# A gated mix of linear attention and a ReLU layer: first x chunk and W1 by plain loads, x transposed on TensorE, and other PSUM banks for nd and finA

## The chip, the cores and the metric

The kernel runs on one core of a Trainium2 chip. A core has five instruction queues that run side by side: TensorE (PE) multiplies matrices, VectorE (DVE), ScalarE (ACT) and GpSimd (POOL) work elementwise, and SyncE (SP) here only issues DMA transfers. ACT and POOL issue some transfers too. A queue works in order: an instruction that waits for a semaphore holds up all that stand behind it. The metric is the device time of one execution in microseconds (us); the runs of a kernel are summed up by their median.

## The reference

For x of 2048 rows and 512 columns (bf16) the output is g * a + (1 - g) * b, row by row:

```python
g = _sigmoid((x * gate_w).sum(-1, keepdims=True))
# a: linear attention, 32 heads of width 16
q, k, v = heads(x @ wqkv)
pq, pk = q @ w_phi, k @ w_phi                       # per head
phi_q = concat(softmax(pq), softmax(-pq))           # 32 features per head
phi_k = concat(softmax(pk), softmax(-pk))
kv, z = phi_k^T @ v, sum_s(phi_k)                   # over all 2048 rows
a = ((phi_q @ kv) / (phi_q . z + 1e-6)) @ wo
# b: dense layer
b = relu(x @ w1) @ w2                               # inner width 1376
```

The sums kv and z go over all rows, so no output row of a can be made before the last row of x has been through the first half.

## The kernel before

The 2048 rows are 16 tiles of 128 (index m), or 4 chunks of 512 (index c). XT holds x transposed, in four slabs of 128 columns of x (index s or dt); HT holds relu(x @ w1) transposed, in 10 full slabs of 128 (index kt) and a remainder of 96.

The order of the work on every engine is written out by hand. A small planner (`_Plan`) appends instructions to one list per engine, each with the events that it waits for; nothing is reordered later. PSUM has 8 banks, and the dictionary `free` remembers for each bank which event frees it.

The head. SP issues four transposing loads of chunk 0 (L138, events x00 to x03), then two of the q and k columns of wqkv (L141, wqk0 and wqk1), a plain load of the v columns (L143, wv), and transposing loads of chunks 1 to 3 (L146). ACT issues W1 in five pieces (L151) and a sixth with the columns from 1024 on (L153, w1r). POOL makes small index tiles (L156 to L159), waits for x02 (L160), then fetches w_phi into WPS (L161) and gate_w (L163), and builds the block matrices Wbd from WPS (L166, L170). PE starts with 12 matmuls on constants (L191) and then makes eight units of chunk 0 at once, one per PSUM bank, slab by slab (L206, called from the end of the program). Each unit is a sum of four matmuls with 512 columns; ACT (L200) or DVE (L202) apply the relu. `pre` (L251) multiplies the q and k weights by Wbd, `rest` (L229) makes the 96 remaining columns and the gate, `vtile` (L314) a tile of v.

The middle. For each tile m, `atile` (L267) makes the logits of q and k, ACT exponentiates them (L278), DVE sums and inverts (L282 to L292), POOL normalises (L294 to L301), and a transposing DMA moves phi_q into PHQ. `kv` (L335) adds tile m - 3 to the sums in banks 6 and 7. The units of chunks 1 to 3 (L206) fill PE between them. Six units of chunk 3 are left for after the last attention tile, with the last three `kv` among and behind them; `gate` (L357 to L360) runs on DVE there.

The join and the tail. `kvfin` (L344, L348) moves the sums into KVNZ on DVE. `nd` (L367) multiplies a tile of PHQ by KVNZ into two banks from b0 on, DVE inverts (L373) and divides (L377), and a transposing DMA (L383) moves the tile into OT. `finB` (L392) makes b, 11 matmuls; `finA` (L401) makes a, 4 matmuls, which ACT scales by the gate (L406, into TFA); `comb` (L415) adds them on DVE and stores the tile (L420). The tail's loop at m issues nd(m + 2), finB(m + 1), finA(m), comb(m).

Of the kernel before, what the change touches and what calls it, by code (L numbers as in the profile page):

```python
# [5 lines left out]
ACT = mybir.ActivationFunctionType  # L6
# [51 lines left out]
def bass_gated_mix__linear_kernel_hedgehog__dense_activation_relu__prompt_kernel(  # L58
# [17 lines left out]
    P = 128  # L76
# [16 lines left out]
    with ExitStack() as es:  # L93
# [14 lines left out]
        KVNZ = E(nc.sbuf_tensor("KVNZ", [P, NG, 68], BF16))  # L108
        OT = E(nc.sbuf_tensor("OT", [P, NDT, S], BF16))
        HR = E(nc.sbuf_tensor("HR", [P, 2, 4, P], BF16))  # L110
        ROW8 = E(nc.sbuf_tensor("ROW8", [P, 8], I32))
        COL8 = E(nc.sbuf_tensor("COL8", [P, 8], I32))
        ROW64 = E(nc.sbuf_tensor("ROW64", [P, 64], I32))
# [9 lines left out]
        TFA = E(nc.sbuf_tensor("TFA", [P, 2, D], BF16))  # L123
        PS = E(nc.psum_tensor("PS", [P, 8, 512], FP32))

        WQKT = PHQ[:, :, S - 512:S]
        OTM = WQK[:, 0, 0:3 * D].rearrange("p (a b) -> p a b", a=3)
        OSB = WQK[:, 1, 0:3 * D].rearrange("p (a b) -> p a b", a=3)
# [5 lines left out]
        free = {b: [] for b in range(8)}  # L134


        for s in range(NDT):
            p.dma("sp", lambda e, s=s: e.dma_start_transpose(  # L138
                out=XT[:, s, 0:512], in_=x2[0:512, s * P:(s + 1) * P]), f"x0{s}", ev=f"x0{s}")
        for i in range(2):  # L140
            p.dma("sp", lambda e, i=i: e.dma_start_transpose(  # L141
                out=WQKT[:, 4 * i:4 * i + 4, :], in_=A_wqkv[:, i * D:(i + 1) * D]), f"wqk{i}", ev=f"wqk{i}")
# [6 lines left out]
        w1parts = [(0, 0, 512), (0, 512, 1024), (1, 0, 1024), (2, 0, 1024), (3, 0, 1024)]  # L149
        for i, (s, a, b) in enumerate(w1parts):  # L150
            p.dma("act", lambda e, s=s, a=a, b=b: e.dma_start(  # L151
                out=W1[:, s, a:b], in_=B_w1[s * P:(s + 1) * P, a:b]), f"w1{i}", ev=f"w1{i}")
        p.dma("act", lambda e: e.dma_start(  # L153
            out=W1[:, :, 1024:DFF], in_=B_w1[:, 1024:DFF].rearrange("(j p) n -> p j n", p=P)), "w1r", ev="w1r")
# [6 lines left out]
        p.dma("pool", lambda e: e.dma_start(  # L161
            out=WPS[:, :, :], in_=A_w_phi.rearrange("(g hl) r c -> (hl r) g c", g=NDT)), "wps", ev="wps")
        p.dma("pool", lambda e: e.dma_start(  # L163
# [5 lines left out]
        for gt in range(NDT):  # L169
# [3 lines left out]
                M8[:, :].unsqueeze(2).to_broadcast([P, 8, FE]), ALU.mult),  # L173
                after=["wd", "m8"], ev=f"wbd{gt}")

        p.op("dve", lambda e: e.tensor_single_scalar(ROW8[:, :], ROW8[:, :], 4, ALU.arith_shift_right),
             after=["iota"], ev="r8")
        p.op("dve", lambda e: e.tensor_single_scalar(ROW64[:, :], ROW64[:, :], 5, ALU.arith_shift_right), ev="r64")
        p.op("dve", lambda e: e.tensor_tensor(M8[:, :], ROW8[:, :], COL8[:, :], ALU.is_equal), after=["r8"], ev="m8")
        p.op("dve", lambda e: e.tensor_tensor(M32[:, :], ROW64[:, :], COL16[:, :], ALU.is_equal),  # L180
             after=["r64"], ev="m32")
        for b in range(NB):
            p.op("dve", lambda e, b=b: e.memset(
                EB[:, b, 0:3, :].rearrange("p a (g f) -> p (a g) f", f=DH)[:, :, FE:DH], 1.0), ev=f"cst{b}")
            p.op("dve", lambda e, b=b: e.memset(VS[:, b, :, 64:65], 1.0), ev=f"one{b}")
        for b in range(2):
            p.op("dve", lambda e, b=b: e.memset(HR[:, b, :, NR:P], 0.0), ev=f"hz{b}")


        for _ in range(12):  # L190
            p.op("pe", lambda e: e.matmul(PS[:, 7, :], ones[:, 0:P], ones, start=True, stop=True))  # L191

        def xready(c):
            return [f"x0{s}" for s in range(NDT)] if c == 0 else [f"x{c}"]

        def relu(c, kt, bank, eng):
            dst, src = HT[:, kt, c * 512:(c + 1) * 512], PS[:, bank, :]
# [7 lines left out]
        def hmm(c, kt, bank, s, after):  # L205
            p.op("pe", lambda e: e.matmul(  # L206
                PS[:, bank, :], W1[:, s, kt * P:(kt + 1) * P], XT[:, s, c * 512:(c + 1) * 512],
                start=(s == 0), stop=(s == NDT - 1)),
                after=after, ev=(f"h{c}_{kt}" if s == NDT - 1 else None))

        rot = [0]

        def nextbank():
            rot[0] += 1
            return 3 + (rot[0] - 1) % 3

        def hunit(c, kt, eng="act"):
            bank = nextbank()
            w = [f"w1{i}" for i in range(len(w1parts))] if kt < 8 else ["w1r"]
            for s in range(NDT):  # L220
                hmm(c, kt, bank, s, (xready(c) + w + free[bank]) if s == 0 else ())
            relu(c, kt, bank, eng)

        def rest(c):
            bank = nextbank()
            for i in range(4):
                for s in range(NDT):
                    t0 = c * 512 + i * P
                    p.op("pe", lambda e, i=i, s=s, t0=t0: e.matmul(  # L229
                        PS[:, bank, i * P:i * P + NR + 1], XT[:, s, t0:t0 + P], W1[:, s, KU * P:DFF + 1],  # L230
                        start=(i == 0 and s == 0), stop=(s == NDT - 1), skip_group_check=True),
                        after=(xready(c) + ["w1r", "gw"] + free[bank] if i == 0 and s == 0 else ()),
                        ev=(f"h{c}_r" if i == 3 and s == NDT - 1 else None))
            src = PS[:, bank, :].rearrange("p (i n) -> p i n", i=4)
            b = c % 2
            p.op("act", lambda e: e.activation(HR[:, b, :, 0:NR], src[:, :, 0:NR], ACT.Relu),
                 after=[f"h{c}_r"] + ([f"hr{c - 2}"] if c >= 2 else []), ev=f"rr{c}")
            p.op("act", lambda e: e.activation(
                EG[:, 4 * c:4 * c + 4].unsqueeze(2), src[:, :, NR:NR + 1], ACT.Exp, scale=-1.0), ev=f"eg{c}")
            free[bank] = [f"eg{c}"]  # L240
            p.dma("sp", lambda e: e.dma_start_transpose(
                out=HT[:, KU, c * 512:(c + 1) * 512].rearrange("p (i t) -> p i t", i=4),
                in_=HR[:, b, :, :].rearrange("p i n -> p (i n)")), f"hr{c}", after=[f"rr{c}", f"hz{b}"], ev=f"hr{c}")

# [116 lines left out]
                 after=["g"], ev="gt")  # L361

        def nd(m):
            b0 = 0 if m == 0 or m % 2 else 2
            after = [f"tq{m}", "kvz1"] + free[b0] + free[b0 + 1]
            for g in range(NG):
                p.op("pe", lambda e, g=g: e.matmul(  # L367
                    PS[:, b0 + g // 4, (g % 4) * GW:(g % 4) * GW + 68],
                    PHQ[:, g, m * P:(m + 1) * P], KVNZ[:, g, :], start=True, stop=True),
                    after=(after if g == 0 else ()), ev=(f"nd{m}" if g == NG - 1 else None))  # L370
            r = m % 2
            ob = m % 3
            p.op("dve", lambda e: e.reciprocal(  # L373
                RDEN[:, r, :].rearrange("p (g h) -> p g h", g=NG),
                bass.AP(tensor=PS, offset=b0 * 512 + 64, ap=[[EPS, P], [GW, NG], [1, HG]])),
                after=[f"nd{m}"], ev=f"rd{m}")
            p.op("dve", lambda e: e.tensor_tensor(  # L377
                OTM[:, ob, :].rearrange("p (g h d) -> p g h d", g=NG, h=HG),
                bass.AP(tensor=PS, offset=b0 * 512, ap=[[EPS, P], [GW, NG], [DH, HG], [1, DH]]),
                bass.AP(tensor=RDEN, offset=r * H, ap=[[2 * H, P], [HG, NG], [1, HG], [0, DH]]), ALU.mult),  # L380
                after=[f"rd{m}"] + ([f"to{m - 3}"] if m >= 3 else []), ev=f"om{m}")
# [29 lines left out]
        def comb(m, cs=slice(0, 512), tag="", eng="sp"):  # L411
            ob = m % 3
            bank = fbank[(m, tag)]
            n = cs.stop - cs.start
            p.op("dve", lambda e: e.scalar_tensor_tensor(  # L415
                out=OSB[:, ob, cs], in0=PS[:, bank, 0:n], scalar=OMG[:, m:m + 1],
                in1=TFA[:, m % 2, cs], op0=ALU.mult, op1=ALU.add),
                after=[f"fb{m}{tag}", f"ta{m}"] + ([f"out{m - 3}"] if m >= 3 else []), ev=f"cb{m}{tag}")
            free[bank] = [f"cb{m}{tag}"]
            p.dma(eng, lambda e: e.dma_start(out=o2[m * P:(m + 1) * P, cs], in_=OSB[:, ob, cs]),  # L420
                  f"out{ob}{tag}", after=[f"cb{m}{tag}"], ev=f"out{m}{tag}")
# [12 lines left out]
        rest(0)  # L434
        vtile(0, "dve")
        for i in range(4, 8):
            pre(i)
        vtile(1, "dve")
# [113 lines left out]
```

## Time and profile before

| | us |
|---|---|
| median of 4 runs | 157.27 |
| lowest to highest | 157.04 to 157.61 |
| the profiled execution | 157.04 |
| its span, first to last instruction | 155.1 |
| PE busy | 145.2 (94%) |
| DVE busy | 89.9 (58%) |
| ACT busy | 71.7 (46%) |
| POOL busy | 55.2 (36%) |

The profile shows one execution. Its table of slices cuts the span into 40 equal parts of 3.88 us; a digit is the busy share in tenths. The chain of work that ended last is followed back from the last instruction to what released it, step by step; a line of it gives the start in us, the duration in us, the engine, the tile and the line of the kernel. The timeline gives start, duration, engine, line, operation, output and input, and in brackets how long the engine had stood idle and for whom. Matmuls overlap: the mean duration of one (379 ns with 512 columns) is longer than the distance between two (0.215 us). PEld is the loading of a matmul's stationary operand, beside the matmuls. A row of a table by windows gives the stretch, its length, the busy time of PE, PEld, DVE, ACT and POOL with the number of instructions, the granted clock of PE, the busy share of the DMA engines, and GB/s.

When the transfers of the head were issued and had landed, in us:

| transfer | KB | issued | landed |
|---|---|---|---|
| x00, x01, x02, x03 (transposing) | 128 each | 0.7, 2.0, 3.3, 4.6 | 4.0, 8.1, 11.4, 11.6 |
| W1, five pieces | 128, 128, 256, 256, 256 | 0.8 to 2.7 | 2.9 to 9.2 |
| w1r | 352 | 3.4 | 11.1 |
| wqk0, wqk1 (transposing) | 512 each | 5.9, 11.2 | 13.9, 16.9 |
| WV | 512 | 13.7 | 18.3 |
| x1, x2, x3 (transposing) | 512 each | 14.4, 18.2, 20.3 | 20.5, 23.9, 25.5 |

### The profile page before, as it was taken

How to read it: one execution, taken by the hardware profiler on the slowest of the kernel's cores; microseconds unless marked ns; L12 is line 12 of the kernel's file. 1: busy time of each engine (PE TensorE's matmuls, PEld its weight loads, DVE VectorE, ACT ScalarE, POOL GpSimd, SP SyncE). 2: the span in 40 equal slices, each digit the busy share in tenths (PEclk: the TensorE clock that was granted, in tenths of full speed). 3: DMA queues.
4: the chain of work that ended last, by engine and by line, in shares of the span. 5: the costliest groups of instructions: out<-in, count | busy, mean ns of one | idle time of the engine just before them, and what ended most of it. 6: DMA issues, size and time to landing. Idle time of an engine off the chain costs nothing.

```text
span 155.1 us, 2475 instructions
## 1 busy us (share of the span) xinstructions
PE 145.2 (94%) x950; PEld 71.9 (46%) x967; DVE 89.9 (58%) x146; ACT 71.7 (46%) x111; POOL 55.2 (36%) x63
## 2 busy tenths in 40 slices
PE   7959699999999999999999999699999999999973
PEld 3323464444544544444554545344454444444432
DVE  2204370878886876868678893744444555554432
ACT  0304456777777777878777763011122211111150
POOL 1004400587866876878877881000000000000000
PEclk9999999999999999999999999999999999999999
DMA  5999996032449686423244432143233322333222
GB/s 132 208 215 222 263 178 135 0 68 68 39 100 277 165 216 86 68 68 70 68 72 101 98 71 68 34 87 86 72 68 88 81 68 68 72 80 90 68 68 68
DMA packets 46602, 16.09 MB, mean 104 GB/s; under 512 B 40976, under 2 KB 46208, under 8 KB 46592
## 3 DMA queue, kind: packets, MB, share of 16 engines
q1 hardware_dynamic: 45136, 14.49, 43.8%
q10 hardware_dynamic: 1392, 1.44, 4.5%
q8 instruction: 7, 0.11, 0.3%
q0 software_dynamic: 64, 0.02, 0.1%
q14 instruction: 3, 0.02, 0.1%
HBM read 3.88 MB, written 2.10 MB: 39 GB/s over the span
## 4 chain that ended last, share of the span: by engine, by line
PE 81%; DMA 5%; ACT 4%; issue 3%; POOL 2%; SPq 2%; DVE 1%; POOLq 0%
PE PS L392 24%; PE PS L267 17%; PE PS L206 15%; PE PS L401 9%; PE PS L314 7%; DMA XT<-in_A_x_dram 5%; ACT EB L278 4%; PE PS L367 3%; PE PS L335 2%; SPq L138 2%; PE PS L229 1%; PE PS L251 1%; POOL Wbd L170 1%; DVE WQK L415 1%; POOL WPS L161 1%
## 5 line engine op out<-in xcount | busy, mean ns | idle before, releaser
L392 PE MATMUL PS<-W,HT 128*128 128x512 bf16 (+4 forms) x181 | 39.8, 366 | 0.3
L206 PE MATMUL PS<-XT,W 128*128 128x512 bf16 x155 | 37.9, 380 | 2.1 <-DMA XT<-in_A_x_dram 1.6
L294 POOL TENSOR_TENSOR EB<-EB,SC 128x1024 bf16<-128x1024 bf16 x16 | 30.8, 1928 | 22.8 <-DVE SC L285 22.8
L278 ACT ACTIVATE EB<-PS 128x960 bf16<-128x960 f32 x32 | 29.4, 970 | 15.5 <-PE PS L267 15.5
L406 ACT ACTIVATE TFA<-PS,GT 128x512 bf16<-128x512 f32 x16 | 11.0, 687 | 45.4 <-PE PS L401 45.4
L267 PE MATMUL PS<-WQK,XT 128*128 128x480 bf16 x128 | 28.6, 367 | 0.5 <-ACT EB L278 0.4
L282 DVE TENSOR_REDUCE ZB<-EB 128x64 f32<-128x1024 bf16 x16 | 19.5, 1220 | 15.7 <-ACT EB L278 15.7
L415 DVE SCALAR_TENSOR_TENSOR WQK<-PS,OMG,TFA 128x512 bf16<-128x512 f32 (+2 forms) x17 | 12.2, 719 | 27.3 <-ACT TFA L406 26.2
L200 ACT ACTIVATE HT<-PS 128x512 bf16<-128x512 f32 x36 | 21.1, 607 | 12.4 <-PE PS L206 12.3
L206 PEld LDWEIGHTS PS<-XT,W 128*128 128x128 bf16 x160 | 15.2, 98 | 20.7 <-DMA XT<-in_A_x_dram 2.6
L392 PEld LDWEIGHTS PS<-W,HT 128*128 128x128 bf16 (+1 forms) x187 | 16.9, 97 | 16.9
L267 PEld LDWEIGHTS PS<-WQK,XT 128*128 128x128 bf16 x128 | 11.9, 98 | 15.4 <-ACT EB L278 3.4
L287 DVE TENSOR_REDUCE ZB<-EB 128x64 f32<-128x1024 bf16 x16 | 18.6, 1161 | 0.0
L301 POOL TENSOR_TENSOR EB<-EB,SC 128x512 bf16<-128x512 bf16 x16 | 16.9, 1055 | 1.3
L401 PE MATMUL PS<-WO,OT 128*128 128x512 bf16 x63 | 16.2, 378 | 0.9 <-ACT TFA L406 0.9
L314 PE MATMUL PS<-WV,XT 128*128 128x512 bf16 x59 | 15.3, 378 | 0.4 <-issue 0.2
L377 DVE TENSOR_TENSOR WQK<-PS,RDEN 128x512 bf16<-128x512 f32 x16 | 11.1, 692 | 0.5
L401 PEld LDWEIGHTS PS<-WO,OT 128*128 128x128 bf16 x64 | 6.2, 97 | 8.7 <-issue 1.3
L285 DVE RECIPROCAL SC<-ZB 128x64 f32<-128x64 f32 x16 | 8.8, 553 | 0.5
L324 ACT ACTIVATE VS<-PS 128x512 bf16<-128x512 f32 x14 | 8.5, 605 | 0.0
L367 PEld LDWEIGHTS PS<-KVNZ,PHQ 128*128 128x128 bf16 x128 | 6.0, 97 | 4.7 <-issue 1.4
L367 PE MATMUL PS<-KVNZ,PHQ 128*128 128x68 bf16 x128 | 6.5, 194 | 1.3 <-DVE WQK L377 1.3
(43 smaller groups left out, 73.0 us busy)
## 6 DMA issues: line engine op xcount, KB each, us to landing
out_dram<-WQK SPq DMA_DIRECT2D x15, 128.0 KB, 1.7
W<-in_B_w_dram ACTq DMA_DIRECT2D x3, 256.0 KB, 5.8
W<-in_B_w_dram SPq DMA_DIRECT2D x1, 768.0 KB, 4.9
WV<-in_A_wqkv_dram SPq DMA_DIRECT2D x1, 512.0 KB, 4.6
W<-in_B_w_dram SPq DMA_DIRECT2D x1, 512.0 KB, 5.9
WO<-in_A_wo_dram SPq DMA_DIRECT2D x1, 512.0 KB, 3.8
W<-in_B_w_dram ACTq DMA_DIRECT2D x1, 352.0 KB, 7.7
W<-in_B_w_dram ACTq DMA_DIRECT2D x2, 128.0 KB, 2.4
```

The lines of the kernel that those rows point to most:

```text
L200: p.op("act", lambda e: e.activation(dst, src, ACT.Relu), after=[f"h{c}_{kt}"], ev=ev)
L206: p.op("pe", lambda e: e.matmul(PS[:, bank, :], W1[:, s, kt * P:(kt + 1) * P], XT[:, s, c * 512:(c + 1) * 512], start=(s == 0), stop=(s == ...
L267: p.op("pe", lambda e, dt=dt, which=which: e.matmul(PS[:, which, 0:DE], XT[:, dt, m * P:(m + 1) * P], WQK[:, which, dt * DE:(dt + 1) * DE] ...
L278: p.op("act", lambda e, s=s, o=dsts[s]: e.activation(o, src, ACT.Exp, scale=(1.0 if s == 0 else -1.0)), after=[f"qk{m}"] + busy, ev=f"{nm} ...
L282: p.op("dve", lambda e: e.tensor_reduce(ZB[:, b, 64:128], EB[:, b, 2, :].rearrange("p (g f) -> p g f", f=DH), AX.X, ALU.add), after=[f"em{ ...
L287: p.op("dve", lambda e: e.tensor_reduce(ZB[:, b, 0:64].rearrange("p (h s) -> p h s", s=2), bass.AP(tensor=EB, offset=base, ap=[[EBS, P], [ ...
L294: p.op("pool", lambda e: e.tensor_tensor(EB[:, b, 3, :].rearrange("p (g f) -> p g f", f=DH), EB[:, b, 2, :].rearrange("p (g f) -> p g f", ...
L301: p.op("pool", lambda e: e.tensor_tensor(EB[:, b, 0, :].rearrange("p (h s f) -> p h s f", h=H, s=2)[:, :, 1, :], EB[:, b, 1, :].rearrange( ...
L314: p.op("pe", lambda e, dt=dt: e.matmul(PS[:, bank, :], XT[:, dt, m * P:(m + 1) * P], WV[:, dt, :], start=(dt == 0), stop=(dt == NDT - 1)), ...
L367: p.op("pe", lambda e, g=g: e.matmul(PS[:, b0 + g // 4, (g % 4) * GW:(g % 4) * GW + 68], PHQ[:, g, m * P:(m + 1) * P], KVNZ[:, g, :], star ...
L392: p.op("pe", lambda e, kt=kt, M=M: e.matmul(PS[:, bank, 0:n], HT[0:M, kt, m * P:(m + 1) * P], W2[0:M, kt, cs], start=(kt == 0), stop=(kt = ...
L401: p.op("pe", lambda e, t=t: e.matmul(PS[:, bank, :], OT[:, t, m * P:(m + 1) * P], WO[:, t, :], start=(t == 0), stop=(t == NDT - 1)), after ...
```

## The change

Chunk 0 of x is fetched by two plain loads on SP into the first columns of OT (under the name XS), which is not written otherwise until the tail. Each partition takes four neighbouring rows of x, so that tile m of the first four holds the rows 4p + m; the stores of these four tiles use the same order (`orow`). PE transposes the 16 blocks with an identity matrix, made by two iotas on POOL and a compare on DVE, into banks 0, 1, 2 and 7; DVE and ACT copy them to XT. W1 comes in four pieces by columns, w10, w11 and w13 on ACT and w12 on SP. SP, and POOL's fetch of WPS and gate_w, then wait for w12; all transposing loads stand behind that wait. PE runs 6 constant matmuls in place of 12.

The first four units of chunk 0 are made in two halves of 256 columns, the other six one after the other as whole units, their relus by ACT and DVE in turn. The tile v0 comes ahead of `rest`.

In the tail, kv of the last tile and `kvfin` come two units earlier, nd(0) comes ahead of finB(0) and nd(1) behind it, nd(2) behind finB(1); nd takes banks 0 and 1 for even tiles and 2 and 3 for odd ones; finA takes bank 6, but 2 and 0 for the last two tiles.

```diff
-        for s in range(NDT):
-            p.dma("sp", lambda e, s=s: e.dma_start_transpose(
-                out=XT[:, s, 0:512], in_=x2[0:512, s * P:(s + 1) * P]), f"x0{s}", ev=f"x0{s}")
+        xq = x2[0:512, :].rearrange("(p j) d -> p j d", j=4)
...
+        for i in range(2):
+            p.dma("sp", lambda e, i=i: e.dma_start(out=XS[:, 2 * i:2 * i + 2, :], in_=xq[:, 2 * i:2 * i + 2, :]),
+                  f"x0{i}", ev=f"x0{i}")
+        w1cuts = [0, 256, 512, 1024, DFF]
+
+        def load_w1(eng, i):
+            a, b = w1cuts[i], w1cuts[i + 1]
+            p.dma(eng, lambda e: e.dma_start(
+                out=W1[:, :, a:b], in_=B_w1[:, a:b].rearrange("(j p) n -> p j n", p=P)), f"w1{i}", ev=f"w1{i}")
+
+        load_w1("act", 0)
+        load_w1("act", 1)
+        load_w1("sp", 2)
+        load_w1("act", 3)
+        p.wait("sp", ["w12"])
...
-        p.wait("pool", ["x02"])
+        p.wait("pool", ["w12"])
...
+        for _ in range(6):
+            p.op("pe", lambda e: e.matmul(PS[:, 7, :], ones[:, 0:P], ones, start=True, stop=True))
...
+        for j in range(4):
+            bank = (0, 1, 2, 7)[j]
+            tp = PS[:, bank, :].bitcast(BF16)[:, 0:512]
+            for dt in range(NDT):
+                p.op("pe", lambda e, tp=tp, j=j, dt=dt: e.transpose(
+                    tp[:, dt * P:(dt + 1) * P], XS[:, j, dt * P:(dt + 1) * P], IDN[:, :]),
+                    after=["idn", f"x0{j // 2}"], ev=(f"xt{j}" if dt == NDT - 1 else None))
...
-        for _ in range(12):
-            p.op("pe", lambda e: e.matmul(PS[:, 7, :], ones[:, 0:P], ones, start=True, stop=True))
...
         def nd(m):
-            b0 = 0 if m == 0 or m % 2 else 2
+            b0 = 2 * (m % 2)
...
-        for s in range(NDT):
-            for u in range(8):
-                w = f"w1{s + 1}" if s else f"w1{u // 4}"
-                hmm(0, u, u, s, [f"x0{s}", w])
-                if s == NDT - 1:
-                    relu(0, u, u, ("act", "dve")[u % 2])
-        hunit(0, 8)
-        hunit(0, 9)
+        for hf in range(2):
+            for u in range(4):
+                hmm(0, u, 3 + u, slice(hf * 256, hf * 256 + 256), [f"xc{2 * hf}", f"xc{2 * hf + 1}"] + w1of(u),
+                    f"h0_{u}" if hf else None)
+        for u in range(4):
+            relu(0, u, 3 + u, ("act", "dve")[u % 2])
+        for u, bank in zip(range(4, KU), (7, 0, 1, 3, 4, 5)):
+            hunit(0, u, ("act", "dve")[u % 2], bank)
         for i in range(4):
             pre(i)
+        vtile(0, "dve")
         rest(0)
-        vtile(0, "dve")
...
+            if i == 4:
+                kv(NT - 1)
+                kvfin()
             unit(*u)
-        kv(NT - 1)
-        kvfin()
+        nd(0)
         finB(0, 4)
-        nd(0)
         nd(1)
...
-            if m + 2 < NT:
+            if 2 <= m + 1 < NT - 1:
                 nd(m + 2)
             if m + 1 < NT - 1:
                 finB(m + 1, FB[(m + 1) % 3])
-            finA(m, 6 if m < NT - 1 else 2)
+            if m == 0:
+                nd(2)
+            finA(m, (6, 2, 0)[max(m - NT + 3, 0)])
```

More of the change, by code (lines that the diff above doesn't have):

```diff
@@ L110, in bass_gated_mix__linear_kernel_hedgehog__dense_activation_relu__prompt_kernel @@
         HR = E(nc.sbuf_tensor("HR", [P, 2, 4, P], BF16))
+        ROWI = E(nc.sbuf_tensor("ROWI", [P, P], I32))
+        COLI = E(nc.sbuf_tensor("COLI", [P, P], I32))
+        IDN = E(nc.sbuf_tensor("IDN", [P, P], BF16))
         ROW8 = E(nc.sbuf_tensor("ROW8", [P, 8], I32))
@@ L124, in bass_gated_mix__linear_kernel_hedgehog__dense_activation_relu__prompt_kernel @@
         PS = E(nc.psum_tensor("PS", [P, 8, 512], FP32))
+        XS = OT[:, :, 0:512]
         WQKT = PHQ[:, :, S - 512:S]
@@ L134, in bass_gated_mix__linear_kernel_hedgehog__dense_activation_relu__prompt_kernel, with orow @@
         free = {b: [] for b in range(8)}
-        for s in range(NDT):
-            p.dma("sp", lambda e, s=s: e.dma_start_transpose(
-                out=XT[:, s, 0:512], in_=x2[0:512, s * P:(s + 1) * P]), f"x0{s}", ev=f"x0{s}")
+        xq = x2[0:512, :].rearrange("(p j) d -> p j d", j=4)
+        oq = o2[0:512, :].rearrange("(p j) d -> p j d", j=4)
+        def orow(m):
+            return oq[:, m, :] if m < 4 else o2[m * P:(m + 1) * P, :]
+        for i in range(2):
[11 more added lines that the diff above has]
+        p.wait("sp", ["w12"])
         for i in range(2):
@@ L147, in bass_gated_mix__linear_kernel_hedgehog__dense_activation_relu__prompt_kernel @@
                 out=XT[:, :, c * 512:(c + 1) * 512], in_=x2[c * 512:(c + 1) * 512, :]), f"x{c}", ev=f"x{c}")
[L149 to L154, printed above, removed]
+        p.op("pool", lambda e: e.iota(COLI[:, :], [[1, P]], channel_multiplier=0))
+        p.op("pool", lambda e: e.iota(ROWI[:, :], [[0, P]], channel_multiplier=1), ev="iota0")
         p.op("pool", lambda e: e.iota(ROW8[:, :], [[0, 8]], channel_multiplier=1))
@@ L174, in bass_gated_mix__linear_kernel_hedgehog__dense_activation_relu__prompt_kernel @@
                 after=["wd", "m8"], ev=f"wbd{gt}")
+        p.op("dve", lambda e: e.tensor_tensor(IDN[:, :], ROWI[:, :], COLI[:, :], ALU.is_equal),
+             after=["iota0"], ev="idn")
         p.op("dve", lambda e: e.tensor_single_scalar(ROW8[:, :], ROW8[:, :], 4, ALU.arith_shift_right),
@@ L181, in bass_gated_mix__linear_kernel_hedgehog__dense_activation_relu__prompt_kernel, with xready @@
              after=["r64"], ev="m32")
+        for _ in range(6):
+            p.op("pe", lambda e: e.matmul(PS[:, 7, :], ones[:, 0:P], ones, start=True, stop=True))
+        def xready(c):
+            return [f"xc{j}" for j in range(4)] if c == 0 else [f"x{c}"]
+        for j in range(4):
[5 more added lines that the diff above has]
+                    after=["idn", f"x0{j // 2}"], ev=(f"xt{j}" if dt == NDT - 1 else None))
+            src = tp.rearrange("p (a b) -> p a b", a=NDT)
+            dst = XT[:, :, j * P:(j + 1) * P]
+            if j % 2 == 0:
+                p.op("dve", lambda e, s=src, d=dst: e.tensor_copy(d, s), after=[f"xt{j}"], ev=f"xc{j}")
+            else:
+                p.op("act", lambda e, s=src, d=dst: e.activation(d, s, ACT.Copy), after=[f"xt{j}"], ev=f"xc{j}")
+            free[bank] = [f"xc{j}"]
         for b in range(NB):
@@ L187, in bass_gated_mix__linear_kernel_hedgehog__dense_activation_relu__prompt_kernel, with w1of @@
             p.op("dve", lambda e, b=b: e.memset(HR[:, b, :, NR:P], 0.0), ev=f"hz{b}")
-        for _ in range(12):
-            p.op("pe", lambda e: e.matmul(PS[:, 7, :], ones[:, 0:P], ones, start=True, stop=True))
-        def xready(c):
-            return [f"x0{s}" for s in range(NDT)] if c == 0 else [f"x{c}"]
+        def w1of(kt):
+            return [f"w1{i}" for i in range(4) if w1cuts[i] <= kt * P < w1cuts[i + 1]]
         def relu(c, kt, bank, eng):
@@ L203, in relu @@
             free[bank] = [ev]
[L205 to L209, printed above, removed]
         rot = [0]
@@ L215, in nextbank, with hmm, hunit @@
             return 3 + (rot[0] - 1) % 3
-        def hunit(c, kt, eng="act"):
-            bank = nextbank()
-            w = [f"w1{i}" for i in range(len(w1parts))] if kt < 8 else ["w1r"]
+        def hmm(c, kt, bank, cols, after, ev):
             for s in range(NDT):
-                hmm(c, kt, bank, s, (xready(c) + w + free[bank]) if s == 0 else ())
+                p.op("pe", lambda e, s=s: e.matmul(
+                    PS[:, bank, cols], W1[:, s, kt * P:(kt + 1) * P],
+                    XT[:, s, c * 512 + cols.start:c * 512 + cols.stop],
+                    start=(s == 0), stop=(s == NDT - 1)),
+                    after=(after if s == 0 else ()), ev=(ev if s == NDT - 1 else None))
+        def hunit(c, kt, eng="act", bank=None):
+            bank = nextbank() if bank is None else bank
+            hmm(c, kt, bank, slice(0, 512), xready(c) + w1of(kt) + free[bank], f"h{c}_{kt}")
             relu(c, kt, bank, eng)
@@ L231, in rest @@
                         start=(i == 0 and s == 0), stop=(s == NDT - 1), skip_group_check=True),
-                        after=(xready(c) + ["w1r", "gw"] + free[bank] if i == 0 and s == 0 else ()),
+                        after=(xready(c) + ["w13", "gw"] + free[bank] if i == 0 and s == 0 else ()),
                         ev=(f"h{c}_r" if i == 3 and s == NDT - 1 else None))
@@ L419, in comb @@
             free[bank] = [f"cb{m}{tag}"]
-            p.dma(eng, lambda e: e.dma_start(out=o2[m * P:(m + 1) * P, cs], in_=OSB[:, ob, cs]),
+            p.dma(eng, lambda e: e.dma_start(out=orow(m)[:, cs], in_=OSB[:, ob, cs]),
                   f"out{ob}{tag}", after=[f"cb{m}{tag}"], ev=f"out{m}{tag}")
-        for s in range(NDT):
-            for u in range(8):
-                w = f"w1{s + 1}" if s else f"w1{u // 4}"
-                hmm(0, u, u, s, [f"x0{s}", w])
-                if s == NDT - 1:
-                    relu(0, u, u, ("act", "dve")[u % 2])
-        hunit(0, 8)
-        hunit(0, 9)
+        for hf in range(2):
[6 more added lines that the diff above has]
+            hunit(0, u, ("act", "dve")[u % 2], bank)
         for i in range(4):
             pre(i)
+        vtile(0, "dve")
         rest(0)
-        vtile(0, "dve")
         for i in range(4, 8):
```

## The prediction

> **What bounds the kernel now.** I read the table of slices first, then the chain of work that ended last in order of time, then the timeline where the chain leaves TensorE (PE). From 24 to 94 us and from 98 to 147 us PE never stops, and nothing there is edited; so the time can only be won or lost in the three thin places.
>
> ```profile
> PE   7959699999999999999999999699999999999973
> DMA  5999996032449686423244432143233322333222
> ```
>
> The head is the first six slices of 3.88 us: PE is partly idle while the DMA row stands at 9. The chain says what it waits for:
>
> ```profile
> 3.32 8.10 DMA XT<-in_A_x_dram
> 11.43 0.30 issue
> 11.72 0.91 POOL WPS L161
> ...
> 16.82 1.45 POOL Wbd L170 x4
> 18.27 0.14 issue
> 18.40 1.00 PE PS L251 x16
> ...
> 23.64 1.64 PE PS L267 x8
> ```
>
> The third transposing load of chunk 0 lands at 11.42. GpSimd (POOL) waits for exactly that one (x02) before it fetches WPS, so Wbd is ready at 18.27 and PE starts `pre` at 18.40. From there PE runs with only 0.17 us idle: `pre` 0-3 1.00, `rest` 0.69, V tile 0.86, `pre` 4-7 0.84, gap 0.17, V tile 0.81, h unit 0.86, until the first attention tile at 23.64, which is 5.24 after `pre` began.
>
> The join of the two halves of the kernel, and the end:
>
> ```profile
> 96.95 0.37 DVE RDEN L373
> 97.32 0.02 issue
> 97.34 0.70 DVE WQK L377
> 98.04 0.14 issue
> 98.18 0.67 PE PS L367 x16
> ...
> 147.58 0.70 ACT TFA L406
> 148.28 0.14 issue
> ```
>
> nd(1) writes the banks of nd(0), so PE stands from 96.92 (0.27 of nd(0) from 96.66) to 98.18, 1.26 us, while VectorE (DVE) divides tile 0. Near the end finA(14) shares bank 6 with finA(13) and waits for its eviction: the wait list gives PE 0.87 us there.
>
> **The head, part by part.** *Loads.* The plain loads up to w12 and w13 are 256 KB x 4, 512 and 352 KB: 1.93 MB. The same bytes needed until 11.4 us before: the windows give 218 GB/s from 2.0 to 11.4. Plain weight loads in this trace move faster:
>
> ```profile
> 2.00:11.40 9.40, 7.86 (x26) 2.75 (x24) 1.39 (x12) 1.28 (x1) 0.00 (x0) 1.00 1.15 218
> 48.00:52.00 4.00, 3.94 (x39) 2.38 (x39) 3.48 (x5) 3.09 (x6) 2.73 (x4) 1.00 1.11 354
> ```
>
> (the last column is GB/s; the second window is W2, 1 KB rows, from one queue). The new w10 and w11 have 512-byte rows, which no row of the trace shows, so I bound the rate: 205 GB/s (these 1.93 MB took the 9.4 us before) to 354, and take 325, near the plain row because no load in flight then transposes. Call T the landing of w12: 2.0 (first bytes; 0.74 to 2.0 carried 33 KB) + 1.93/0.325 = 7.9, with its receipt 8.0 (bounds 7.6 and 11.6). The Trainium skill, "DMA: Bandwidth & Descriptors", section "Issuing engines are not separate DMA queues", speaks against a gain from the second queue: all queues share the same 16 DMA engines, and only issue time is saved. The trace agrees: 354 GB/s came from one queue, and the loads before were on two queues already at 218. A sum by "two queues, twice the rate" would put T at 6.5; I leave T at 8.0, on the plain rate alone.
>
> *PE transposes.* x00 shares the engines with w10: 0.52 MB at 292 GB/s, the rate of the window from 2 to 3, is 1.8, so x00 at 3.8 and x01 at about 5.4. The identity costs two 128x128 iotas on POOL and one compare on DVE. The nearest rows are the 128x64 iotas (0.18, 0.19) and the compare of 128x64 (0.23); up to double each, ready by 2.0, hidden behind the load. The warm-ups give PE's cold pace: 12 of 512 columns start from 0.78 to 5.43, 0.423 apart, against 0.215 later (L392: 11 in 2.38). Six end at 3.4. A transpose of 128 columns is then 0.107 cold, 8 are 0.86: j 2 and 3 run from 5.4 to 6.3, where the W1 units can begin. The copies of j 0 and 1 (nearest row: 0.69 on DVE and 0.60 on ACT for 128x512) fit between 4.7 and 5.4; those of j 2 and 3 lie beside the first-half matmuls. The DVE fills of EB and VS, now behind two copies, end near 11.5, before DVE's first relu is wanted.
>
> *W1 units.* 32 matmuls of 256 columns at 0.108 plus 24 of 512 at 0.215 are 8.6 at full pace, as much as the 40 before: 6.3 + 8.6 = 14.9. But PE is cold:
>
> ```profile
> L191 PE MATMUL PS<-const-bfloat16-1.0 x12: 583/631/631, 0.8 to 5.4; 128*128 128x512 bf16 x12
> ```
>
> and L206's first matmul in the same view is 591 ns against a median of 379. The twelve warm-ups were followed by full pace at about 6.3, 5.5 us after they began. The Trainium skill, "TensorE: Matmul & The Clock Gate", Part 1, says the clock doubles after one whole busy window of 3.4 us and that the window runs free of the kernel; Part 4 adds that transposes do not count as busy. Six warm-ups (2.6 us) can't fill a window, so by the rule the units start cold and turn warm between 9.7 and 13.1. The trace shows only the late turn, consistent with a window from 2.9 to 6.3. By the row alone (5.5 us from 0.78, whatever ran) there is no penalty and the units end at 14.9; by the rule they lose half of 3.4 to 6.8 us, ending at 16.6 to 18.3. I take 17.2, nearer the rule, because PE will have stood idle twice in the window.
>
> *What `pre` then needs.* SP holds its transposing loads until T. Held behind that wait are wqk0, wqk1, WV, x1 to x3 and later hr0; POOL's WPS, gw, WD and Wbd wait for T as well. From the rows of 512 KB loads before: issue about 2.5 (L141's unqueued one 2.52), landing 5.2 after issue at best (L146), and then a spacing of 13.9 (25.5 - 11.6) over six loads, about 2.3. So wqk0 lands at T + 5.3 = 13.3, wqk1 at T + 7.9 = 15.9, WV at T + 9.4 = 17.4, x1 at T + 11.5 = 19.5. Wbd: 18.27 was 6.85 after x02, so T + 6.85 = 14.9; gw, 5.2 after, comes at 13.2. PE arrives at `pre` at 17.2 and finds all of it; the V tile, moved ahead of `rest`, is reached at 18.2, 0.8 after WV; the h unit of chunk 1 at 21.6, 2 us after x1. The first attention tile moves from 23.64 to 17.2 + 5.24 = 22.4: **1.2 us saved**. The floor is WV: even a warm PE waits for it at 17.4, then 4.3 of work: 21.7, at most 1.9 saved.
>
> **The join: 1.1 saved.** kv(15) needs the last GpSimd product, ready at 92.10; moved two units (1.72) earlier PE reaches it at 92.30, a margin of 0.2. kvfin (0.93) then queues behind the gate arithmetic on DVE, free at 93.47:
>
> ```profile
> 90.17 1.93 POOL L294 TENSOR_TENSOR EB<-EB,SC 128x1024 bf16<-128x1024 bf16 x1 [0.45 <-DVE SC L285]
> ...
> 92.45 1.02 DVE L360 TENSOR_SCALAR OMG<-GT 128x16 f32<-128x16 f32 x1
> ```
>
> so nd(0) can start at about 94.45, where PE is ready at 94.28: a new stall of 0.2. finB(0) (2.38) covers tile 0's division (1.09), and nd(1) has other banks. Removed 1.26, added 0.2.
>
> **The end: 0.25 saved.** With banks 6, 2 and 0, finA(14) follows at once, saving 0.87. What is late next is the transposed tile 15: SP issues it at 146.57 and such a DMA takes 2.4 in all but its contended cases, so 148.97, while finA(15) would be ready at 148.42. A stall of 0.6 is given back. Strided rows of the first four output tiles stay 128 rows of 1 KB, off the path.
>
> **Sum.** 157.04 (span 155.1 and 1.94 around it) - 1.2 - 1.1 - 0.25 = 154.5. The median of the runs is 0.23 above the profiled execution, so **154.7**.
>
> **Rivals.** *A, as worked out:* 154.7, chance 0.50. *B, the head gains nothing:* PE turns warm at 13.1 or later and reaches `pre` at 18.4 again, or WV keeps the V tile waiting; only the tail is left, 157.27 - 1.35 = 155.9. For it speaks the rule on transposes; against it that PE is steadily busy from 6.3. Chance 0.25. *C, warm at once:* PE waits for WV, head 1.9 and to15 a little sooner: 153.8, chance 0.08. *D, the held loads come too late:* at 205 GB/s T is 11.6, WV lands at 21.0, and the first attention tile moves to 25.3, 1.7 later, against 1.35 of tail: 157.6. PE, standing from about 18 to 21, may fall back to the cold pace, up to 1.7 more (half of 3.4): 158.4 in the middle. It decides once T passes 11.3. For it: small rows, and a mean of 218 before 11.4; against it: the 354 of plain loads. Chance 0.17. *That the hold does nothing* is part of A: bytes, not order, set T.
>
> **How the numbers follow.** A measurement of this kernel tells changes from none at about 0.3% (0.5 us). A, B and C are faster: 0.83. D splits into 0.05 within and 0.12 slower. The range is 153.4 (C's gain, with the join a little better) to 157.0 (B with a late WV); what it leaves out is D and a remainder of C.
>
> **What would show it.** Right: w12 landing near 8; W1 units from about 6.3; W1 matmuls of 256 columns about 0.21 apart at first and 0.11 later; `pre` at 16.5 to 17.5 with no wait on Wbd; no DVE piece between the nd tiles near 95; finA(15) waiting for a DMA. Wrong: V tile or `pre` waiting for WV or wqk, w12 after 10, W1 units starting after 7, or kv(15) waiting for GpSimd.

## The result, and the profile after

The changed kernel takes 156.81 us (median of 34 runs) against 157.46 us for the kernel before (55 runs). The ratio is 0.9948, with a 95% interval of 0.9933 to 0.9963: 0.8 us faster, where 2.5 us and 154.7 had been forecast. The ratio is of the fast runs alone: seven runs of the changed kernel and four of the other, more than 1.5% above the fastest of their kernel, are left out of it, and so the medians of all runs lie only 0.65 us apart. That 156.81 lies within the forecast range of 153.4 to 157.0 is luck: the cause was none of the four cases.

The profile shown here is of an execution of 158.39 us, in which TensorE (PE) fell to half its pace at the very end; in most executions it doesn't, and a second profile of the same kernel, after_again, used below, has it at full pace to the end.

The table of slices of the kernel after (40 slices of 3.91 us; PEclk is the granted clock in tenths, 9 being 90% or more):

```profile
PE   6799899999999999999999999999999999999593
PEclk9999999999999999999999999999999999999968
DMA  3949997028249696131324434143332224222611
```

The head is better filled than before (its first six slices read 6, 7, 9, 9, 8, 9 where they had read 7, 9, 5, 9, 6, 9), but the DMA row has a hole in its third slice, and PE now has a 5 in the third slice from the end, with a low clock behind it. Neither had been forecast. The chain of work that ended last, its lines for the head, the join and the end:

```profile
1.76 7.35 DMA W<-in_B_w_dram
9.11 0.02 issue
9.13 2.23 SPq L163
11.36 0.05 issue
11.40 2.42 SPq L163
13.83 0.04 issue
13.87 4.63 DMA WV<-in_A_wqkv_dram
18.50 0.05 issue
18.55 1.04 PE PS L351 x4
...
22.99 1.63 PE PS L304 x8
...
93.79 0.41 PE PS L404 x8
94.20 2.38 PE PS L429 x11
96.58 0.26 PE PS L404 x8
...
144.82 3.95 DMA OT<-WQK
148.77 0.05 issue
148.82 1.04 PE PS L438 x4
149.85 4.10 PE PS L429 x22
```

*Head.* The chain no longer goes through Wbd but through w12 (landed at 9.11), the held transposing loads, and WV at 18.50; PE had finished `pre` 0-3 and stood 0.68 us for it. The first attention tile begins at 22.99 in the chain, 0.65 earlier than before (22.82 in the timeline, which counts from the first matmul's start). *Join.* nd(0) and finB(0) follow one another with no DVE piece between the nd tiles, as forecast. *End.* The transfer of tile 15 into OT, to15, takes 3.95 us from its issue where it took 2.4 before, and finA(15) starts at 148.82. The last 22 matmuls then take 4.25 us in place of 2.57. PE's timeline of the kernel before and of the kernel after:

```profile
150.14 2.57 PE L392 MATMUL PS<-W,HT 128*128 128x384 bf16 x22
```

```profile
149.69 4.25 PE L429 MATMUL PS<-W,HT 128*128 128x384 bf16 x22
```

Where the time went, from the timelines of all profiles (us; a tile whose first matmul is missing from the records is counted from where that matmul belongs, 0.22 earlier). The first column is one execution each and scatters, since it hangs on transfers; the ratios carry the verdicts.

| kernel | first attention tile | from there to finA(0) | from there to the end of PE | PE waits before finA(15) | ratio to before |
|---|---|---|---|---|---|
| before | 23.48 | 77.6 | 51.6 | 0 (finA(14): 0.87) | 1 |
| after | 22.82 | 76.5 | 54.6 | 2.17 | 0.9948 |
| after_again | 23.10 | 76.5 | 52.6 | 1.84 | 0.9974 |
| head_only | 22.65 | 77.6 | 51.6 | 0 (finA(14): 0.87) | 0.9952 |
| tail_only | 24.22 | 76.5 | 51.4 | 0.64 | 0.9904 |
| tail_late | 23.11 | 76.5 | 54.9 | 2.48 | 1.0035 |
| fetch_early | 24.11 | 76.5 | 51.5 | 0.69 | 0.9902 |
| fetch_still | 23.26 | 76.5 | 53.1 | 2.26 | 0.9996 |
| no_hold | 21.84 | 76.5 | 54.9 | 2.47 | 0.9901 |
| no_hold_early | 22.14 | 76.5 | 51.5 | 0.68 | 0.9802 |
| b_first | 21.48 | 76.5 | 50.9 | 0 | 0.9771 |
| best | 21.37 | 76.5 | 50.9 | 0 | 0.9758 |

What made to15 late stands in the view of the DMA queues, cut to the 4 us in which it was in flight (kernel after; a line per queue gives packets, MB, and the share of 16 engines; a line per transfer its count and the us from issue to landing):

```profile
q1 hardware_dynamic: 797, 0.36, 65.6%
q8 instruction: 1, 0.02, 1.9%
out_dram<-WQK SPq DMA_DIRECT2D x2, 128.0 KB, 1.7
OT<-WQK SPq DMA_TRANSPOSE x1, 4.0
```

A single packet of the queue of kind "instruction" runs beside it. Over the whole program this queue had 7 packets before and 8 after, 16 KB each (packets, MB and share of the two pages, before and after), and the eighth falls between 146.0 and 146.5:

```profile
q8 instruction: 7, 0.11, 0.3%
```

```profile
q8 instruction: 8, 0.13, 0.4%
```

So theory F: to15 is late because the code of PE is fetched beside it, and the fetch stands there because the head's edits make PE's program 26 matmuls longer (78 in place of 52). Rival R: the new tail itself makes its transfers collide.

### The profile page after: what moved, and what is told of

It is laid out like the page before. It is cut to its first block, busy times and chain, and to the rows that moved or that the text cites. A ratio compares the mean times of both kernels' runs of the same rounds, so it can differ in the third digit from the quotient of the medians.

```text
span 156.3 us, 2530 instructions
## 1 busy us (share of the span) xinstructions
PE 147.5 (94%) x976; PEld 75.5 (48%) x993; DVE 91.8 (59%) x150; ACT 72.5 (46%) x112; POOL 55.6 (36%) x65
## 4 chain that ended last, share of the span: by engine, by line
PE 73%; DMA 10%; ACT 5%; DVE 5%; SPq 4%; issue 1%
PE PS L429 24%; PE PS L304 17%; PE PS L250 11%; PE PS L438 8%; PE PS L351 7%; ACT EB L315 5%; DMA W<-in_B_w_dram 5%; SPq L163 3%; DMA WV<-in_A_wqkv_dram 3%; PE PS L404 3%; DMA OT<-WQK 3%; PE PS L372 2%; PE PS L266 1%; DVE ZB L319 1%; DVE ZB L324 1%
## 5 line engine op out<-in xcount | busy, mean ns | idle before, releaser
L429 PE MATMUL PS<-W,HT 128*128 128x512 bf16 (+4 forms) x183 | 41.8, 378 | 0.2
L250 PE MATMUL PS<-XT,W 128*128 128x512 bf16 (+1 forms) x170 | 39.0, 372 | 0.3
L429 PEld LDWEIGHTS PS<-W,HT 128*128 128x128 bf16 (+1 forms) x187 | 17.5, 101 | 18.0 <-issue 1.7
L250 PEld LDWEIGHTS PS<-XT,W 128*128 128x128 bf16 x176 | 17.6, 103 | 16.7 <-DMA XT<-in_A_x_dram 0.5
L351 PEld LDWEIGHTS PS<-WV,XT 128*128 128x128 bf16 x64 | 5.4, 97 | 5.3 <-DMA WV<-in_A_wqkv_dram 0.8
```

Of the source, the lines that this page charges most:

```text
L250: p.op("pe", lambda e, s=s: e.matmul(PS[:, bank, cols], W1[:, s, kt * P:(kt + 1) * P], XT[:, s, c * 512 + cols.start:c * 512 + cols.stop], ...
L351: p.op("pe", lambda e, dt=dt: e.matmul(PS[:, bank, :], XT[:, dt, m * P:(m + 1) * P], WV[:, dt, :], start=(dt == 0), stop=(dt == NDT - 1)), ...
L429: p.op("pe", lambda e, kt=kt, M=M: e.matmul(PS[:, bank, 0:n], HT[0:M, kt, m * P:(m + 1) * P], W2[0:M, kt, cs], start=(kt == 0), stop=(kt = ...
```

## The experiments

**The tail alone.** The kernel before, with the edits to kv, kvfin, nd and finA only, none to loads, transposes or units:

```diff
-            b0 = 0 if m == 0 or m % 2 else 2
+            b0 = 2 * (m % 2)
...
-            finA(m, 6 if m < NT - 1 else 2)
+            finA(m, (6, 2, 0)[max(m - NT + 3, 0)])
```

> The kernel before with the tail's edits alone (kv and kvfin two units earlier, the order and banks of nd, banks 6, 2, 0 of finA); TensorE's program has as many instructions as before. Theory F (in the changed kernel the transfer of tile 15 into OT, to15, is late because a 16 KB code fetch of TensorE runs at 146.0 to 147.3, beside it; the fetch stands there because the head's edits add 26 matmuls to TensorE's program): no fetch near to15, which lands 2.4 us after its issue; join 1.05 and end 0.25 saved, 1.3 us in all, ratio to before 0.992. Rival R (the tail's own new order makes to15 collide with the stores of tiles 12 and 13): to15 takes about 4 us here too, finA(15) waits about 2.2 us, and at most 0.4 us are saved, ratio 0.997 to 1.000.

Ratio 0.9904 (0.9878 to 0.9931). The DMA view of this kernel over the 4 us from the issue of to15 has no packet of the instruction queue, and to15 lands after 2.4:

```profile
q1 hardware_dynamic: 794, 0.35, 33.0%
out_dram<-WQK SPq DMA_DIRECT2D x2, 128.0 KB, 1.7
OT<-WQK SPq DMA_TRANSPOSE x1, 2.4
```

The timeline of PE gives the wait that is left, 0.64 (0.6 was forecast):

```profile
148.69 1.04 PE L401 MATMUL PS<-WO,OT 128*128 128x512 bf16 x4 [0.64 <-DMA OT<-WQK]
```

Rival R falls: the new tail alone is worth more (1.5 us) than the whole change (0.8).

**The tail, and a longer program.** The same with 28 matmuls on constants behind the 12 of the start, where PE then waits for x anyway:

```diff
+        for _ in range(28):
+            p.op("pe", lambda e: e.matmul(PS[:, 7, 0:64], ones[:, 0:P], ones[:, 0:64], start=True, stop=True))
```

> The kernel before with the tail's edits, as tail_only, and 28 constant matmuls of 64 columns behind its 12 of the start. They end about 1.5 us later, before the second and third slab of x have landed (8.1 and 11.4 us), so the head should not move; but TensorE's eighth code fetch now comes near to15. Theory F: to15 takes 3.6 to 4 us, finA(15) waits about 2.2 us in place of 0.64, 1.5 us more than tail_only, ratio to before 1.000 in place of 0.990. Rival: matmuls that hide behind a load cost nothing wherever they move the fetch, 0.990.

Ratio 1.0035 (1.0010 to 1.0060), 0.0131 or 2.1 us more than without them. The head didn't get longer (first tile at 23.11), but now an eighth fetch stands at 146.0 to 146.5, and the DMA view around to15 reads:

```profile
q1 hardware_dynamic: 796, 0.36, 64.0%
q8 instruction: 1, 0.02, 2.4%
out_dram<-WQK SPq DMA_DIRECT2D x2, 128.0 KB, 2.0
OT<-WQK SPq DMA_TRANSPOSE x1, 4.3
```

In PE's timeline the same four matmuls wait 2.48 in place of 0.64:

```profile
149.41 1.59 PE L403 MATMUL PS<-WO,OT 128*128 128x512 bf16 x4 [2.48 <-DMA OT<-WQK]
```

Matmuls that do nothing and lie beside a load cost as much as the new tail had won: theory F. Only PE's program was made longer here, and the fetch came; so the packets of this queue are PE's code. The excess over the 1.5 forecast is the clock: in this execution too the granted clock fell to 0.50 (from about 149.7 to 153.2 us), and the mean clock shows such a fall in 8 of the 22 runs; the 14 others have a median of 157.42, beside 157.43 for the kernel before, which is the 1.000 of the forecast.

**The changed kernel with the fetch moved.** 12 matmuls of 64 columns, and as a control 3, behind the 6 of the start:

```diff
         for _ in range(6):
             p.op("pe", lambda e: e.matmul(PS[:, 7, :], ones[:, 0:P], ones, start=True, stop=True))
+        for _ in range(12):
+            p.op("pe", lambda e: e.matmul(PS[:, 7, 0:64], ones[:, 0:P], ones[:, 0:64], start=True, stop=True))
```

> The changed kernel with 12 more constant matmuls of 64 columns behind the 6 of the start, in the time in which TensorE waits for the first half of x (3.5 to 4.3 us). They add 24 instructions, so each code fetch comes about 12 matmuls (some 2.6 us) earlier in the tail, at about 143.4 to 144.7, between the transfers of tiles 14 and 15. Theory F: to15 lands 2.4 us after its issue, finA(15) waits about 0.6 us in place of 2.2; 1.5 us less than the changed kernel, ratio to before about 0.985. Rival R: nothing of the tail changes, ratio 0.995 as for the changed kernel, or more where the added matmuls cost time.

> The same with 3 constant matmuls of 64 columns: the fetch moves by about 0.6 us only and still meets to15. Theory F: to15 takes 3.3 to 4 us, ratio to before 0.993 to 0.996, as the changed kernel. Rival R2 (added matmuls gain by warming TensorE in the head, wherever the fetch stands): part of the gain of the run with 12 shows here too.

With 12 the last fetch moved to 142.5, to15 landed after 2.5, and finA(15) waited 0.69: the mechanism as expected. The time, 0.9902 (0.9870 to 0.9935), was 0.8 us short of it. In the profiled execution, the slowest of the six (156.68; the median is 156.08), WV landed late (PE waited 1.1) and x1 at 23.2 (0.6), and the first tile began at 24.11: what was gained at the end was lost again in the head, where the first fetch now stood at 20.3 beside x1. That the other five lost less of the same kind is likely, but not shown. With 3 the fetch stayed (146.5 to 147.0, to15 issued at 145.25) and the wait was 2.26; the ratio, 0.9996 (0.9956 to 1.0036), is even above that of the changed kernel, with runs from 156.5 to 159.7: the clock fell in 6 of the 12, and the 6 others have a median of 156.89, 0.9945 of the kernel before. So added matmuls as such gain nothing. The first tile's scatter, 22.65 to 24.11 in the kernels with the hold, suggests that the head had a problem of its own.

**The head alone.** The changed kernel with the old tail:

> The changed kernel with the tail as before: the head's edits alone, 26 more matmuls in TensorE's program than before. In the old tail finA(14) waits 0.87 us for ACT, so finA(15) comes later and covers part of a late to15. Theory F + H: first attention tile 0 to 0.8 us earlier, by when WV and x1 land (18.5 to 19.2 and 21.9 to 23.2 in the three runs with the hold); the fetch comes at about the end of to15's transfer and costs 0 to 0.7; ratio 0.996 to 1.001. As forecast before (head 1.2 us): 0.992.

Ratio 0.9952 (0.9934 to 0.9970), 0.76 us: a little better than the 0.996 to 1.001 expected, at the upper end of theory H, and not the 1.2 us of the forecast. The first tile began at 22.65, with a wait of 0.7 for WV. The fetch came at 148.5, when to15 (issued at 145.74) had landed, and cost nothing. Together the two halves alone make 0.0048 + 0.0096 = 0.0144; both at once measured 0.0052. The missing 0.0092, 1.4 us, is the fetch that neither half has at that place, and the fall of the clock behind it: no run of head_only or tail_only shows one, of 28.

**The hold taken away.** The changed kernel without SP's wait; POOL still waits for w12:

```diff
         load_w1("act", 3)
-        p.wait("sp", ["w12"])
```

> The changed kernel without SP's wait for w12; POOL's wait for w12 stays. Theory H (the hold leaves the DMA engines empty for some 2 us, from 8.4 to 10.7 us in the profile, and so WV lands at 18.5 and x1 at 21.9, for which TensorE waits 0.7 and 0.5 us): w12 still lands near 9, wqk0, WV and x1 about 2 us earlier, both waits go, the first attention tile starts about 0.9 us earlier, ratio 0.995 - 0.006 = 0.989 to before. Rival B (the order of the transfers doesn't matter, or the transposing loads push W1 back): W1 lands 1 us or more later, TensorE waits for w12 or w13 among the W1 units, ratio 0.995 or more.

Ratio 0.9901 (0.9871 to 0.9931), with the late to15 still in it (a wait of 2.47). The table by windows of the kernel after and of this one, for the same 2.3 us (the last column is GB/s):

```profile
8.40:10.70 2.30, 2.30 (x16) 1.78 (x15) 0.64 (x6) 0.12 (x1) 1.29 (x2) 1.00 0.06 17
```

```profile
8.40:10.70 2.30, 2.30 (x21) 1.95 (x19) 0.76 (x6) 0.42 (x1) 0.93 (x2) 1.00 1.28 258
```

With the hold the DMA engines move 17 GB/s while SP waits for w12's receipt and then for its first transposing load to start; without it 258. w12 landed 0.36 us later (at 9.47), not the 1 us or more of rival B, and PE waits for no W1 piece among the units. WV was issued at 12.3 in place of 13.9, no wait of PE for WV or x1 is left, and the first tile begins at 21.84. Rival B falls.

**Both causes removed.** The 12 small matmuls and no hold:

> The changed kernel without SP's wait for w12 and with 12 constant matmuls of 64 columns in the gap at the start. If both causes stand and add up: head 1.6 us (first attention tile at 22.0 as in no_hold), join 1.05, end 0.25, 2.9 us in all, and finA(15) waits 0.65 us: ratio to before about 0.981. If the two runs before shared one cause, 0.990 as each of them.

Ratio 0.9802 (0.9775 to 0.9829), 3.1 us faster than before. Both marks are there, the first tile at 22.14 and a wait of 0.68 before finA(15), so these are two causes and not one. Against the changed kernel's 0.9948 this is 0.0146, more than the 0.0046 and 0.0047 that the two edits brought alone: the run with 12 matmuls had lost time in the head, and no_hold still had the late to15.

**The changed kernel again,** beside the last three on one chip:

> The changed kernel itself, beside the others on one chip: ratio 0.993 to 0.997; TensorE's eighth code fetch near 146, to15 landing 3.6 to 4 us after its issue, a wait of about 2.2 us before finA(15), WV landing at 18.5 to 19.2.

Ratio 0.9974 (0.9940 to 1.0008), within the interval's reach of the first. Its DMA view around to15, and PE's wait:

```profile
q8 instruction: 1, 0.02, 1.2%
out_dram<-WQK SPq DMA_DIRECT2D x2, 128.0 KB, 1.7
OT<-WQK SPq DMA_TRANSPOSE x1, 3.6
```

```profile
148.77 1.04 PE L438 MATMUL PS<-WO,OT 128*128 128x512 bf16 x4 [1.84 <-DMA OT<-WQK]
```

The clock stayed up here (0.999 over the span), so the late transfer is no product of the execution shown above; the fall of the clock is a second price on it. The mean clock of every run is on record: it is below 0.995 in 27 of the 89 runs of kernels whose to15 is late (after, after_again, tail_late, fetch_still, no_hold), and in 4 of 126 of the others, the kernel before among them.

**A better version.** First the small piece of finB(15) into the wait that is left; then, besides, 8 matmuls of 512 columns and 8 of 64 at the start, and 2 of 512 between the groups of transposes:

```diff
+            if m == NT - 1:
+                finB(m, 3, slice(384, 512), "b")
             finA(m, (6, 2, 0)[max(m - NT + 3, 0)])
...
-        for i, cs in enumerate(cuts):
-            finB(m, (4, 3)[i], cs, "ab"[i])
-        for i, cs in enumerate(cuts):
-            comb(m, cs, "ab"[i], ("sp", "act")[i])
+        finB(m, 4, cuts[0], "a")
+        comb(m, cuts[1], "b", "act")
+        comb(m, cuts[0], "a", "sp")
```

> no_hold_early with the small last piece of finB(15) (128 columns, 11 matmuls, about 0.6 us) ahead of finA(15), where TensorE waits 0.68 us for to15, and its combination and store ahead of the large piece. The matmuls fill the wait; the last combination is the 384-column one, 0.62 us: 0.4 to 0.6 us less than no_hold_early, ratio to before 0.977. If the end is set by the stores or by DVE instead, 0.980 as before.

> b_first with 8 constant matmuls of 512 columns and 8 of 64 at the start, and 2 of 512 between the two groups of transposes, so that TensorE is busy from 0.8 to 6.5 us and turns to its full pace near 6.3 as in the kernel before. The W1 units take 8.7 to 9.2 us in place of 9.8, TensorE reaches pre at 16.3 and the first attention tile at about 21.7 in place of 22.3: ratio 0.974 to 0.976. If the clock turns as late as without the fillers (the transposes not counting as work), 0.977 to 0.979.

0.9771 (0.9745 to 0.9797) and 0.9758 (0.9732 to 0.9785). The second took 153.96 us (median of 5) beside 157.64 for the kernel before, 2.4% faster. Its last matmuls in PE's timeline run without a wait:

```profile
145.04 0.78 PE L433 MATMUL PS<-W,HT 128*128 128x128 bf16 x11
145.89 1.04 PE L442 MATMUL PS<-WO,OT 128*128 128x512 bf16 x4
146.76 1.95 PE L433 MATMUL PS<-W,HT 128*128 128x384 bf16 x11
```

What the fillers add to the reordering is not told apart: the intervals overlap, and both first tiles (21.48 and 21.37) begin after a wait of 1.2 of `pre`, in both cases until Wbd is there. Wbd still hangs on POOL's wait for w12; a kernel without that wait was not run.

## Why the prediction was wrong, step by step

**The join: right.** 1.1 us forecast; from the first attention tile to finA(0) it is 77.6 before and 76.5 after, in every kernel with the new tail.

**The end: the step that failed.** "SP issues it at 146.57 and such a DMA takes 2.4 in all but its contended cases." The sum was sound wherever 2.4 holds: tail_only waits 0.64, and from finA(0) to PE's end it saves 0.2, as forecast. But to15 is a contended case in the changed kernel, 3.6 to 4.0 us. The trace of before had the warning in it: its seven packets of the instruction queue, and one transfer into OT that took 4.2. I had taken these for nothing, because before, every late transfer into OT had slack. The edit that I called a saving (finA(14) not waiting for ACT) took away what slack the last one had (0.3 us: it landed at 148.97, and finA(15) began at 149.28); the edit that I counted only by its time in the head (26 more matmuls) is what brought a fetch there. None of the four cases held this. The end cost about 1 us (52.6 against 51.6) where 0.25 was to be saved, and 3 where the clock fell as well. The sign named beforehand, finA(15) waiting for a DMA, came true with 2.17 or 1.84 in place of 0.6. With 0.7 from the head, 1.1 from the join and 1.0 lost at the end, the account closes at 0.8.

**The head: right mechanism, T mis-sized.** T was to be 8.0 and was 9.11. The rate was well chosen: from 4.0 to 8.4 the windows give 334 GB/s against the 325 assumed, and the 334 came over two queues, no more than the 354 of one: the Trainium skill's rule in "DMA: Bandwidth & Descriptors", section "Issuing engines are not separate DMA queues", is in agreement. What failed is the start and the end of the sum. Only 169 and 254 GB/s flowed in the third and the fourth us (the last column; windows of the kernel after):

```profile
2.00:3.00 1.00, 1.00 (x4) 0.29 (x2) 0.28 (x3) 0.60 (x1) 0.00 (x0) 1.00 0.63 169
3.00:4.00 1.00, 0.50 (x2) 0.00 (x0) 0.00 (x0) 0.69 (x1) 0.00 (x0) 1.00 0.90 254
4.00:8.40 4.40, 3.65 (x25) 2.92 (x26) 1.23 (x5) 1.19 (x2) 0.00 (x0) 1.00 1.08 334
```

And the last bytes moved at about 8.6, 0.5 us ahead of w12's semaphore, for which 0.1 was set. From T on, WV hit its offset (T + 9.4 = 18.5, landed at 18.50), in part by luck: wqk0 came 0.2 later and wqk1 1.0 earlier than theirs. x1 came 1.3 later than its T + 11.5 = 20.6; it took 7.4 us from its issue. In all twelve profiles the time of x1 goes with the first code fetch: where the fetch falls into its flight, well ahead of the landing, x1 takes 7.4 to 8.4 us (after, after_again, fetch_early, b_first), where it falls at the landing or behind it, 5.7 to 6.1 (the other eight). No run moved that fetch alone. PE was at `pre` at 16.86, 0.3 ahead of the forecast, and then stood for WV, a sign of being wrong that had been named; so the cold pace took nothing, and WV was the floor that the working had named. after_again confirms it: at full pace from its first transposes on, it waited 1.04 at `pre` and 1.24 for WV, and its first tile came no earlier (23.10). The 1.2 of the sum was 0.66 in this profile and 0.76 by head_only.

**The hold.** I wrote that bytes, not order, set T. That is so, and it misled: order set what came after T. The 2.3 us of idle DMA engines were inside my offset of 5.3 us for wqk0, as a cost, and I never asked what the sum would be without it. no_hold answers: 1 us at the first tile (21.84 against 22.82).

**The clock in the head.** By the rule of the Trainium skill ("TensorE: Matmul & The Clock Gate", Part 1) the units were to turn to full pace between 9.7 and 13.1. The kernel after did so near 9.9: its matmuls of 256 columns start 0.213 us apart up to 9.8 and 0.109 apart from 10.0 on. (PEclk reads 1.00 throughout the head; the cold pace shows only in these distances.) The row of before, taken alone, would have had 6.3. Other executions of the same kernel turned far earlier (below), so no forecast of this to better than 1.5 us is to be had from one trace.

## What to carry to other kernels

A program's length is a quantity of the kernel: each 16 KB of TensorE's code is fetched by the same DMA engines that carry the data, so an edit at the start can move a fetch onto the last transfer that somebody waits for. Look for packets of the instruction queue around any transfer with no slack, before and after an edit, and when two changes that won alone don't add up. A wait that holds transfers back to give others the engines costs the receipt and the restart, 2.3 us of nearly idle DMA engines here; without it w12, issued ahead of them in the same queue, landed only 0.36 us later.

## What was unexpected of the hardware

A fetch of 16 KB keeps one DMA engine of 16 busy for 0.9 to 2.0 us, but to15 beside it lands 1.2 to 1.9 us late (3.6 to 4.3 in place of 2.4): after its bulk, 5 to 10 GB/s trickle on until it lands. Transfers with slack hide this: in no_hold_early the transfer of tile 14 takes 3.3 us beside a fetch, and nobody waits. The Trainium skill ("Runtime: NRT & Kernel Launch", section "Instruction fetch mechanics") tells of refills in blocks of 16 KiB and calls their cost mostly hidden; here one of them, in the wrong place, cost 1.3% of the kernel (tail_late against tail_only, the falls of the clock included).

After an idle time of 2.17 us the clock fell in the execution above (the table by windows of the kernel after; the third figure from the end is the granted clock):

```profile
150.00:152.00 2.00, 2.00 (x8) 0.91 (x7) 0.00 (x0) 0.58 (x1) 0.00 (x0) 0.50 0.00 0
```

After 1.84 us in after_again and 2.26 in fetch_still it did not, so the length of the wait does not decide alone. In the three profiles with a fall (after, tail_late, no_hold) it came 0.3 to 1.0 us after the matmuls had begun again, and the clock stayed at 0.50 for 3.4 us. The Trainium skill ("TensorE: Matmul & The Clock Gate", Part 1) gives an idle window of about 3.4 us for it, in windows that run free of the kernel. The 3.4 us agrees as the length of the fall; as an idle time that must pass it does not.

In the head the full pace came early in some executions, with no more work than six matmuls, or six and a few small ones. PE's timeline of b_first and of no_hold_early, which have the same start:

```profile
6.44 8.84 PE L251 MATMUL PS<-XT,W 128*128 128x256 bf16 x56
```

```profile
7.28 10.06 PE L251 MATMUL PS<-XT,W 128*128 128x256 bf16 x55
```

8.84 is full pace for all 56 matmuls of the units; the 10.06 hold some 2.5 us at half pace. In b_first the second group of transposes, at 5.98, ran at full pace already, and in fetch_still and after_again the first one (at 4.65 and 4.46), after less than 3 us of work and about 1 us of waiting. The same page of the skill gives one busy window of about 3.4 us; these turns lie earlier than a window that is busy throughout would allow.
